# A first chunk of keys ahead of the query weights: reordering and splitting loads in a one-core decode kernel

## The chip, the cores and the metric

The kernel runs on one core of a Trainium2 chip. The metric is the device time of one execution, in microseconds; several runs are made and their median is given. The core has engines that run side by side, each with an instruction list of its own: PE (matrix products), DVE (vector work), ACT (activations), POOL, and SP, which here does nothing but issue transfers. Sixteen DMA engines move the data between HBM and the on-chip memory. They are fed by queues, and a queue works its transfers off in the order in which they were issued.

## The reference: one decode step of a transformer block

The input is a single token, `x` of 512 values. The step is attention over a long cache and then a gated feed-forward layer, each on the normalized input and added to it:

```
q = layernorm(x) @ wq                       # 32 query heads of 128
scores = q . k / sqrt(128)                  # 8 key heads, each serves 4 query heads, 65536 keys
o = softmax(scores) . v
h = x + o @ wo                              # wq is 512 x 4096, wo is 4096 x 512
out = h + (sigmoid(g) * u) @ w_down         # g, u = layernorm(h) @ w_gate, @ w_up ; F = 1792
```

All data are bf16. The keys and values of one head are 16 MiB each, 256 MiB for the eight heads. There is one query token, so each byte of the cache is read once and used for four query heads.

## The kernel before: how the work is tiled and staged

The cache of a head is cut into 32 *chunks* of 2048 keys, 512 KB each; `CH` is the length of one chunk in a partition. A chunk has 128 partitions with 16 keys of 128 values in each. Chunks live in a buffer called `ring`, which has room for 36 of them. A head's keys come in two halves, chunks 0 to 15 and 16 to 31 (`PIECES`), and so do its values. In a load of one half, partition p holds 256 keys that follow each other in memory, so its row is 64 KB long; which key lies in which partition and chunk follows from that (`rows` in `load`, L337). Keys and values must agree on this, since the weights of the softmax come out in the order of the keys.

`load(k, h, q, deps, sem, name, cols)` issues one transfer on SP's queue: head h, half q, chunks `cols` of it. `deps` are what SP waits for before it issues, `sem` the semaphore that counts the landing, `name` what others wait for. SP's list begins with wq (L341), which goes into `ktw`, and the keys of head 0 in four transfers of eight chunks (K0.0a, K0.0b, K0.1a, K0.1b). The first DMA in SP's list is placed ahead of the entry code of the program (L195 to L202). Then, for h from 1 to 7, come K*h*.0, V*(h-1)*.0, K*h*.1, V*(h-1)*.1, each waiting until its part of the ring is free: the marks `F` of DVE (L534) say that keys are used up, the names `PV` of PE that values are.

For each chunk DVE transposes the keys from `ring` into one of eight buffers in `ktw` (L531), and PE multiplies them with the head's query weights (`head_weights`, L500, a copy that ACT makes into the last part of `ktw`). Since wq lies in `ktw` too, the first transposes wait until the projection of the queries has read it. Within a head the chunks are taken in the order `ORDER = (*range(4, 16), *range(4), *range(16, 32))`. PE's four score matrices of a head stay in PSUM; `softmax(h)` has DVE find the maxima, ACT the exponentials (L577) and, as the last step, ACT copies the query weights of head h+1. The copy counts on a semaphore of its own ("W"), and PE's first scores of head h+1 wait for it. PE's work on the values of head h (`pv`) runs between the score blocks of head h+1; it waits for `V{h}.0` and `V{h}.1`. PE and DVE run the heads in loops, so the waits inside must be alike for all heads; ACT's and SP's lists are written out in full.

After the last head come the output projection and the feed-forward layer, whose weights are loaded into the same buffers at the end of SP's list (L354 to L374).

Of the kernel before, what the change touches and what calls it, by code (L numbers as in the profile page):

```python
# [9 lines left out]
AF = mybir.ActivationFunctionType  # L10
# [10 lines left out]
TC = 16  # L21
# [14 lines left out]
class Prog:  # L36
# [14 lines left out]
    def op(self, eng, fn, deps=(), name=None, to=None, times=1):  # L51
        assert name is None or name not in self.where, name
        self.ops[eng].append(dict(fn=fn, deps=[d for d in deps if d], name=name, dma=None, to=to, times=times, part=self.part.get(eng)))
        if name:
            self.where[name] = (eng, len(self.ops[eng]) - 1)

    def dma(self, eng, fn, sem, deps=(), name=None):
        self.op(eng, fn, deps, name)
        rec = self.dma_sems.setdefault(sem, dict(sem=None, count=0))
        rec["count"] += 16  # L60
        self.ops[eng][-1]["dma"] = (sem, rec["count"])
# [162 lines left out]
def bass_sequential_preLN__gqa_block_cached__glu_gated_glu__decode_kernel(  # L224
# [10 lines left out]
    CH = TC * DH  # L235
    PIECES = ((0, 16), (16, 32))
# [10 lines left out]
    with ExitStack() as es:  # L247
        def sb(name, shape, dt):
            return es.enter_context(nc.sbuf_tensor(name, shape, dt))
# [14 lines left out]
        ring = sb("ring", [128, RING], bf16)  # L264
# [4 lines left out]
        qz = sb("qz", [128, 8 * 64], bf16)  # L269
# [45 lines left out]
        def ps(bank, c0, c1, p0=0, p1=128):  # L315
            return PS[p0:p1, bank * 512 + c0: bank * 512 + c1]
# [5 lines left out]
        op, dma = P.op, P.dma  # L322
# [7 lines left out]
        def first_chunk(k, h, q):  # L330
            return AT[{("K", 0): "K0", ("V", HKV - 1): "V7"}.get((k, h), k)][q]

        def load(k, h, q, deps, sem, name, cols=None):
            j0, j1 = PIECES[q]
            a, z = cols or (j0, j1)
            cache = A_k_cache if k == "K" else A_v_cache
            rows = cache[0, h, j0 * TC * 128:j1 * TC * 128, :].rearrange("(p t) d -> p (t d)", p=128)  # L337
            at = (first_chunk(k, h, q) - j0) * CH
            dma("sp", lambda e: e.dma_start(ring[:, at + a * CH:at + z * CH], rows[:, (a - j0) * CH:(z - j0) * CH]), sem, deps, name)  # L339

        dma("sp", lambda e: e.dma_start(ktw[:, 0:NKT * CH].rearrange("p (k n) -> p k n", k=4),  # L341
                                        A_wq.rearrange("(p k) n -> p k n", p=128)), "r0", (), "wq")
        for q in range(2):
            for i in range(2):
                j0 = 16 * q + 8 * i
                load("K", 0, q, (), f"r{2 * q + i + 1}", f"K0.{q}{'ab'[i]}", (j0, j0 + 8))
        for h in range(1, HKV):
            load("K", h, 0, ["F0.0" if h == 1 else f"F{h - 1}.1"], "ka", f"K{h}.0")
            load("V", h - 1, 0, ["F0.1" if h == 1 else f"PV{h - 2}.3"], "va", f"V{h - 1}.0")
            load("K", h, 1, [f"F{h}.0"], "kb", f"K{h}.1")  # L350
            load("V", h - 1, 1, [f"PV{h - 1}.1"], "vb", f"V{h - 1}.1")
        h = HKV - 1
# [11 lines left out]
        for k, w in (("wg", B_w_gate), ("wu", B_w_up)):  # L364
            src = w.rearrange("(p k) n -> p (k n)", p=128)
            for i, (k0, k1) in enumerate(W_SPLIT[k]):
                at = W_AT[k]
                dma("sp", lambda e, at=at, w=src, a=k0 * FF, z=k1 * FF: e.dma_start(ring[:, at + a:at + z], w[:, a:z]),  # L368
                    f"{k}{i}", [f"PV{HKV - 1}.1"] if k == "wg" else (), f"{k}.{i}")
        src = B_w_down.rearrange("(p r) n -> p r n", p=128)  # L370
        for i, (r0, r1) in enumerate(WD_SPLIT):
            at = AT["wd"] * CH
# [123 lines left out]
        def head_weights(h):  # L496

            dst = bass.AP(tensor=ktw, offset=W0 + NC - 1, ap=[[KTW_ROW, 128], [WJ, 4], [NC, 16]])
            src = bass.AP(tensor=qz, offset=64 * h, ap=[[512, 128], [16, 4], [1, 16]])
            op("act", lambda e: e.activation(dst, src, AF.Copy), ["qz", "Wz"] if h == 0 else (), f"W{h}", to="W")  # L500

        def clear_out(h):

            op("act", lambda e: e.activation(ps(PO, 0, 512), bass.AP(tensor=zcol, offset=0, ap=[[1, 128], [0, 512]]), AF.Copy),  # L504
               ["zcol"] if h == 0 else (), f"z{h}", to="po")

        head_weights(0)
        clear_out(0)

# [4 lines left out]
        def dve_block(b):  # L514
            h, r = b // NR, b % NR
            for c in range(NC):
                n, s = b * NC + c, r * NC + c
                j = ORDER[s]
                q = sum(j >= z for _, z in PIECES)
                at = (first_chunk("K", h, q) + j - PIECES[q][0]) * CH  # L520
                src = ring[:, at:at + CH].bitcast(fp32)
                dst = ktw[:, (n % NKT) * CH:(n % NKT + 1) * CH].bitcast(fp32)
                if h == 0:
                    deps = [f"K0.{q}{'ab'[j % 16 // 8]}"] if s in (0, 4, 16, 24) else []
                    if s == 0:
                        deps.append("q")
                else:
                    deps = [f"K{h}.{q}"] if s in (0, 16) else []
                if r:
                    deps.append(f"S{b - 1}.{c}")  # L530
                op("dve", lambda e, d=dst, sr=src: e.transpose(d, sr), deps, f"T{b}.{c}", to="T")  # L531
                mark = ({15: 0, 31: 1} if h == 0 else {11: 0, 27: 1}).get(s)
                if mark is not None:
                    op("dve", lambda e, m=4 * h + mark: e.memset(scr[:, m:m + 1], 0.0), (), f"F{h}.{mark}")  # L534
            if b % NR == NR - 1:
                for k in range(NR):
                    u = b - NR + 1 + k
                    op("dve", lambda e, u=u: e.tensor_reduce(M_sb[:, u % 4:u % 4 + 1], ps(u % NS, 0, 512), AX.X, ALU.max),  # L538
                       [f"S{b}.{NC - NR + k}"], f"mx{u}", to="D")
                op("dve", lambda e: e.memset(scr[:, 32 + b // NR:33 + b // NR], 0.0), (), f"G{b // NR}")  # L540
# [19 lines left out]
        def softmax(h):  # L560
            k = h % 2
            op("dve", lambda e: e.tensor_reduce(gm[:, :], M_sb[:, :], AX.X, ALU.max),
               [f"mx{NR * h + r}" for r in range(NR)], f"gm{h}", to="g")
            op("pe", lambda e: e.matmul(ps(MISC, 0, 128, 0, 1), lhsT=gm[:, :], rhs=identf[:, :], start=True, stop=True),  # L564
               [f"gm{h}"], f"gmT{h}", to="Q")
            op("dve", lambda e: e.tensor_reduce(gmj[:, :], ps(MISC, 0, 128, 0, 1).rearrange("p (i a c) -> p a i c", a=4, c=NC),  # L566
                                                AX.XY, ALU.max), [f"gmT{h}"], f"gmj{h}", to="D")
            op("dve", lambda e: e.tensor_copy(gmrep[:, :].rearrange("p (i a c) -> p i a c", a=4, c=NC),  # L568
                                              bass.AP(tensor=gmj, offset=0, ap=[[4, 1], [0, 4], [1, 4], [0, NC]])),
               [f"gmj{h}"], f"gmrep{h}", to="g")  # L570
            op("pe", lambda e: e.matmul(ps(MISC, 128, 129), lhsT=gmrep[0:1, :], rhs=one_f[0:1, 0:1], start=True, stop=True),  # L571
               [f"gmrep{h}"], f"neg{h}")
            op("act", lambda e: e.activation(negmax[:, k:k + 1], ps(MISC, 128, 129), AF.Copy, scale=-att_scale),  # L573
               [f"neg{h}"], f"negmax{h}")
            for r in range(NR):
                b = NR * h + r
                op("act", lambda e, b=b: e.activation(P_sb[:, (b % 4) * 512:(b % 4 + 1) * 512], ps(b % NS, 0, 512), AF.Exp,  # L577
                                                      bias=negmax[:, k:k + 1], scale=att_scale,
                                                      accum_out=L_sb[:, b % 4:b % 4 + 1]), [f"negmax{h}"],
                   f"E{b}", to="E")  # L580
            if h + 1 < HKV:
                head_weights(h + 1)
# [259 lines left out]
        for i, (nm, bank) in enumerate((("wg", GB), ("wu", UB))):  # L842
            at = W_AT[nm]
# [73 lines left out]
```

## Time and profile before

| | |
|---|---|
| time, median of 3 runs | 656.33 us (656.27 to 656.40) |
| the profiled execution | span of 655.0 us from its first to its last instruction |
| PE busy | 397.5 us (61%) |
| DVE busy | 350.3 us (53%) |
| ACT busy | 43.1 us (7%) |
| moved by DMA | 282.33 MB, mean 431 GB/s over the span |
| mean clock granted to PE | 0.786 of full speed |

The page of the profile gives the busy time of each engine, the transfers, and the chain of work that ended last, followed back from the last instruction. Lines are those of the kernel (L531 is the transposes). "SPq" is SP's sequencer issuing a transfer. A transfer has two times: that of its issue, which is short, and that of its landing, when all its data are there and those who wait for it may go on. The views in order of time give the start of a piece first and then its length; windows give busy time of each engine between two times, the clock granted to PE, the mean share of the DMA engines that was busy, and the rate. All times are in microseconds from the first instruction of the profiled execution.

### The profile page before, as it was taken

Reading aid. Unit: us, or ns where it says so; the run is one execution under the profiler, and the core shown is the slowest. Engines: PE = TensorE matmul, PEld = TensorE weight load, DVE = VectorE, ACT = ScalarE, POOL = GpSimd, SP = SyncE. Lnnn points to the kernel's source line nnn. Section 1 sums busy time; section 2 is a strip of 40 time slices with the busy share of each in tenths; the row PEclk is TensorE's granted clock in tenths of the full one; section 3 lists DMA queues with packets and bytes.
Section 4 is the critical chain, followed back from the end, with each engine's and each line's share of the span. In section 5 each row is a group of like instructions: output and inputs, shape, how many; then the busy total and the mean of one; then the engine's idle time right before and its main releaser. Section 6 shows DMA issues by size and latency. Waiting matters only on the chain.

```text
span 655.0 us, 6176 instructions
## 1 busy us (share of the span) xinstructions
PE 397.5 (61%) x2317; PEld 66.7 (10%) x1549; DVE 350.3 (53%) x428; ACT 43.1 (7%) x114; POOL 3.7 (1%) x19
## 2 busy tenths in 40 slices
PE   2778672937548293674828467392845739285466
PEld 1100010110101000010100101010010101001122
DVE  3398853819266290935719184481917548092202
ACT  1100200020000200002000200002000020001101
POOL 1000000000000000000000000000000000000000
PEclk9799695977959687785968769596796958878656
DMA  9999999999999999999999999999999989999998
GB/s 400 432 434 462 424 408 448 448 448 412 420 448 448 432 400 448 448 448 404 428 448 448 436 396 448 448 448 416 416 448 448 448 384 448 448 448 424 417 412 363
DMA packets 6372, 282.33 MB, mean 431 GB/s; under 512 B 738, under 2 KB 868, under 8 KB 1252
## 3 DMA queue, kind: packets, MB, share of 16 engines
q1 hardware_dynamic: 6340, 282.33, 99.7%
q10 hardware_dynamic: 32, 0.00, 0.0%
HBM read 282.33 MB, written 0.00 MB: 431 GB/s over the span
## 4 chain that ended last, share of the span: by engine, by line
DMA 66%; DVE 30%; PE 2%; issue 1%; SPq 0%; PEldq 0%
DMA ring<-in_A_k_cache_dram 58%; DVE ktw L531 30%; DMA ring<-in_B_w_up_dram 4%; DMA ring<-in_A_v_cache_dram 4%; PE PS L443 2%; PE PS L866 0%; PE PS L847 0%; DVE hh L859 0%; DVE hhT L863 0%; SPq L368 0%; SPq L339 0%; DVE y_sb L884 0%; PEldq L171 0%
## 5 line engine op out<-in xcount | busy, mean ns | idle before, releaser
L531 DVE STREAM_TRANSPOSE ktw<-ring 128x1024 f32<-128x1024 f32 x256 | 291.5, 1208 | 165.0 <-DMA ring<-in_A_k_cache_dram 165.0
L443 PE MATMUL PS<-ktw 128*128 128x512 bf16 x1024 | 276.3, 419 | 163.4 <-DVE ktw L531 155.8
L443 PE MATMUL PS<-ring,PT_sb 128*32 x1024 | 85.0, 420 | 55.0 <-issue 46.6
L443 PEld LDWEIGHTS PS<-ktw 128*128 x256 | 26.2, 102 | 401.5 <-issue 234.3
L618 ACT ACTIVATE po_sb<-PS,rl 128x512 bf16<-128x512 f32 x8 | 5.5, 687 | 523.4 <-PE PS L443 523.4
L443 PEld LDWEIGHTS PS<-ring,PT_sb 128*32 x1024 | 20.7, 116 | 117.5 <-issue 116.2
L566 DVE TENSOR_REDUCE gmj<-PS 1x4 f32<-1x128 f32 x8 | 2.2, 278 | 53.5 <-PE PS L564 53.5
L538 DVE TENSOR_REDUCE M_sb<-PS 128x1 f32<-128x512 f32 x32 | 19.9, 683 | 19.3 <-PE PS L443 19.3
L577 ACT ACTIVATE P_sb<-PS,negmax 128x512 bf16<-128x512 f32 x32 | 21.6, 686 | 0.3
L587 DVE STREAM_TRANSPOSE PT_sb<-P_sb 128x512 bf16<-128x512 bf16 x32 | 19.9, 674 | 1.7 <-ACT P_sb L577 1.7
L443 PE MATMUL PS<-ktw,xz 128*8 x32 | 9.6, 476 | 6.1 <-DMA ktw<-in_A_wq_dram 6.1
L634 DVE TENSOR_TENSOR Lw<-O,blk_of 128x896 bf16<-128x896 bf16 (+1 forms) x2 | 1.4, 682 | 15.9 <-ACT O L624 15.9
L489 DVE STREAM_TRANSPOSE qt<-qh 32x512 bf16<-32x512 bf16 x1 | 0.7, 699 | 14.8 <-ACT qh L486 14.8
L571 PE MATMUL PS<-one_f,gmrep 1*128 1x1 f32 x16 | 4.7, 358 | 5.0 <-DVE gmrep L568 5.0
L564 PE MATMUL PS<-identf,gm 128*1 128x128 f32 x16 | 4.5, 380 | 5.1 <-issue 2.9
L643 DVE CAST O<-PS 128x28 bf16<-128x28 f32 (+1 forms) x2 | 0.3, 174 | 12.8 <-PE PS L640 12.8
L577 ACT ACTIVATION_READ_ACCUMULATOR P_sb<-PS,negmax 128x1 f32 x32 | 6.5, 203 | 0.0
L621 PE MATMUL PS<-sel_bf,po_sb 128*128 128x4 bf16 x32 | 2.1, 170 | 6.3 <-ACT po_sb L618 6.3
L504 ACT ACTIVATE PS<-zcol 128x512 f32<-128x512 bf16 x8 | 5.0, 622 | 0.0
L573 ACT ACTIVATE negmax<-PS 128x1 f32<-128x1 f32 x8 | 1.4, 171 | 54.0 <-PE PS L571 54.0
L571 PEld LDWEIGHTS PS<-one_f,gmrep 1*128 1x128 f32 x16 | 4.0, 307 | 8.8 <-DVE gmrep L568 8.8
L592 PE MATMUL PS<-L_sb,lsel 128*128 128x4 f32 x16 | 2.5, 229 | 3.8 <-DVE PT_sb L587 3.8
(90 smaller groups left out, 65.4 us busy)
## 6 DMA issues: line engine op xcount, KB each, us to landing
ring<-in_A_k_cache_dram SPq DMA_DIRECT2D x4, 4096.0 KB, 34.8
ring<-in_A_v_cache_dram SPq DMA_DIRECT2D x1, 5120.0 KB, 30.1
ktw<-in_A_wq_dram SPq DMA_DIRECT2D x1, 4096.0 KB, 12.2
ktw<-in_A_wo_dram SPq DMA_DIRECT2D x1, 3584.0 KB, 18.4
ring<-in_A_v_cache_dram SPq DMA_DIRECT2D x1, 3072.0 KB, 36.9
ring<-in_B_w_gate_dram SPq DMA_DIRECT2D x1, 1792.0 KB, 23.4
ring<-in_B_w_up_dram SPq DMA_DIRECT2D x1, 1792.0 KB, 27.2
ring<-in_B_w_down_dram SPq DMA_DIRECT2D x1, 1024.0 KB, 29.2
```

Of the source, the lines that this page charges most:

```text
L443: return e.add_instruction(mybir.InstMatmult(name=nc.get_next_instruction_name(), engine=mybir.EngineType.PE, ins=[rhs, lhsT], outs=[e.low ...
L504: op("act", lambda e: e.activation(ps(PO, 0, 512), bass.AP(tensor=zcol, offset=0, ap=[[1, 128], [0, 512]]), AF.Copy), ["zcol"] if h == 0 e ...
L531: op("dve", lambda e, d=dst, sr=src: e.transpose(d, sr), deps, f"T{b}.{c}", to="T")
L538: op("dve", lambda e, u=u: e.tensor_reduce(M_sb[:, u % 4:u % 4 + 1], ps(u % NS, 0, 512), AX.X, ALU.max), [f"S{b}.{NC - NR + k}"], f"mx{u}" ...
L564: op("pe", lambda e: e.matmul(ps(MISC, 0, 128, 0, 1), lhsT=gm[:, :], rhs=identf[:, :], start=True, stop=True), [f"gm{h}"], f"gmT{h}", to="Q")
L566: op("dve", lambda e: e.tensor_reduce(gmj[:, :], ps(MISC, 0, 128, 0, 1).rearrange("p (i a c) -> p a i c", a=4, c=NC), AX.XY, ALU.max), [f" ...
L571: op("pe", lambda e: e.matmul(ps(MISC, 128, 129), lhsT=gmrep[0:1, :], rhs=one_f[0:1, 0:1], start=True, stop=True), [f"gmrep{h}"], f"neg{h}")
L577: op("act", lambda e, b=b: e.activation(P_sb[:, (b % 4) * 512:(b % 4 + 1) * 512], ps(b % NS, 0, 512), AF.Exp, bias=negmax[:, k:k + 1], sca ...
L587: op("dve", lambda e, b=b: e.transpose(PT_sb[:, (b % 4) * 512:(b % 4 + 1) * 512], P_sb[:, (b % 4) * 512:(b % 4 + 1) * 512]), [f"E{b}"], f" ...
L592: op("pe", lambda e: e.matmul(ps(MISC, 132, 136), lhsT=lsel[:, :], rhs=L_sb[:, :], start=True, stop=True), [f"PT{NR * h + NR - 1}"], f"l{h ...
L618: op("act", lambda e: e.activation(po_sb[:, :], ps(PO, 0, 512), AF.Copy, scale=rl[:, :]), [f"PV{h}.{NR - 1}", f"rl{h}"], f"po{h}", to="po")
L621: op("pe", lambda e, t=t: e.matmul(ps(OX, 0, 4), lhsT=po_sb[:, t * 128:(t + 1) * 128], rhs=sel_bf[:, 8 * t:8 * t + 8:2], start=(t == 0), s ...
```

## The change

The first half of head 0's keys is assigned anew: chunk 0 is now the first 2048 keys, one contiguous block of 512 KB with 4 KB in each partition, and chunks 1 to 15 are the 30720 keys behind it, with 60 KB of consecutive keys in each partition. The order within the softmax doesn't matter as long as the values follow, so the first half of head 0's values is assigned in the same way.

Chunk 0 of the keys, `K0.0c`, becomes a transfer of its own and the first in SP's list, ahead of wq. `K0.0a` then has seven chunks (1 to 7) in place of eight. `V0.0` becomes two transfers, `V0.0c` (chunk 0) and `V0.0` (chunks 1 to 15), one right after the other. DVE's transpose of chunk 0 waits for `K0.0c`, and ACT's copy of the query weights of head 1 (`W1`) waits for `V0.0c`.

```diff
             at = (first_chunk(k, h, q) - j0) * CH
-            dma("sp", lambda e: e.dma_start(ring[:, at + a * CH:at + z * CH], rows[:, (a - j0) * CH:(z - j0) * CH]), sem, deps, name)
-
+            c0 = j0
+            if h == q == 0:
+                first = TC * 128
+                c0, keys = (0, (0, first)) if z == 1 else (1, (first, PIECES[0][1] * TC * 128))
+                rows = cache[0, h, keys[0]:keys[1], :].rearrange("(p t) d -> p (t d)", p=128)
+            dma("sp", lambda e: e.dma_start(ring[:, at + a * CH:at + z * CH], rows[:, (a - c0) * CH:(z - c0) * CH]), sem, deps, name)
+
+        load("K", 0, 0, (), "r5", "K0.0c", (0, 1))
         dma("sp", lambda e: e.dma_start(ktw[:, 0:NKT * CH].rearrange("p (k n) -> p k n", k=4),
                                         A_wq.rearrange("(p k) n -> p k n", p=128)), "r0", (), "wq")
         for q in range(2):
             for i in range(2):
                 j0 = 16 * q + 8 * i
-                load("K", 0, q, (), f"r{2 * q + i + 1}", f"K0.{q}{'ab'[i]}", (j0, j0 + 8))
+                load("K", 0, q, (), f"r{2 * q + i + 1}", f"K0.{q}{'ab'[i]}", (max(j0, 1), j0 + 8))
         for h in range(1, HKV):
             load("K", h, 0, ["F0.0" if h == 1 else f"F{h - 1}.1"], "ka", f"K{h}.0")
-            load("V", h - 1, 0, ["F0.1" if h == 1 else f"PV{h - 2}.3"], "va", f"V{h - 1}.0")
+            if h == 1:
+                load("V", 0, 0, ["F0.1"], "vc", "V0.0c", (0, 1))
+            load("V", h - 1, 0, ["F0.1" if h == 1 else f"PV{h - 2}.3"], "va", f"V{h - 1}.0", (1, 16) if h == 1 else None)
...
-            op("act", lambda e: e.activation(dst, src, AF.Copy), ["qz", "Wz"] if h == 0 else (), f"W{h}", to="W")
+            op("act", lambda e: e.activation(dst, src, AF.Copy), ["qz", "Wz"] if h == 0 else ["V0.0c"] if h == 1 else (), f"W{h}", to="W")
...
                     if s == 0:
                         deps.append("q")
+                    if j == 0:
+                        deps.append("K0.0c")
```

## The prediction

> **What bounds the kernel now.** I read the page first, for the share of each engine and for the chain of work that ended last.
>
> ```profile
> span 655.0 us, 6176 instructions
> PE 397.5 (61%) x2317; PEld 66.7 (10%) x1549; DVE 350.3 (53%) x428; ACT 43.1 (7%) x114; POOL 3.7 (1%) x19
> DMA packets 6372, 282.33 MB, mean 431 GB/s; under 512 B 738, under 2 KB 868, under 8 KB 1252
> q1 hardware_dynamic: 6340, 282.33, 99.7%
> DMA 66%; DVE 30%; PE 2%; issue 1%; SPq 0%; PEldq 0%
> ktw<-in_A_wq_dram SPq DMA_DIRECT2D x1, 4096.0 KB, 12.2
> ```
>
> No compute engine is busy for more than 61% of the span, while the one queue that SP feeds keeps the sixteen DMA engines occupied for 99.7% of it. The chain is two thirds DMA. Its other third, DVE, needs a second look: it could mean that DVE sets when transfers are issued and that the queue then runs dry. The chain in order of time shows how the two interlock:
>
> ```profile
> 1.31 30.32 DMA ring<-in_A_k_cache_dram
> 45.34 24.98 DMA ring<-in_A_k_cache_dram
> 84.16 24.75 DMA ring<-in_A_k_cache_dram
> ...
> 108.93 13.67 DVE ktw L531 x13
> ...
> 547.86 24.73 DMA ring<-in_A_k_cache_dram
> 572.61 13.70 DVE ktw L531 x13
> ...
> 621.60 27.22 DMA ring<-in_B_w_up_dram
> ```
>
> The first number is the start, the second the length. A half head of keys (8 MiB) lands, DVE works through enough of it to free the ring, SP issues the next half, and 24.7 to 25.0 us later that one lands. Landings at 70.32 (45.34 + 24.98) and 572.59 (547.86 + 24.73) are 13 such periods apart: 38.64 us for 16 MiB of keys and values, or 434 GB/s. Is that the DMA engines' limit or the loop's? An idle queue answers it. wq, 4 MiB, is the first transfer and lands 12.2 us after its issue. Its bytes at 434 GB/s are 9.66 us, so latency alone is about 2.5 us. Then 8 MiB issued into an empty queue would land after 19.32 + 2.5 = 21.9 us. The keys take at least 24.73, so every issue finds **about 2.9 us of earlier work still queued**. The queue never runs dry, and DVE's 30% are time in which the engines were working off that backlog. The stretches by window say the same:
>
> ```profile
> core 0: us, PE busy (x) PEld busy (x) DVE busy (x) ACT busy (x) POOL busy (x), PEclk, DMA share, GB/s
> 2.75:12.00 9.25, 0.79 (x3) 0.60 (x3) 3.66 (x19) 0.71 (x2) 1.20 (x4) 1.00 1.05 450
> 12.00:30.00 18.00, 12.73 (x40) 3.57 (x35) 5.20 (x5) 3.24 (x7) 0.00 (x0) 0.86 0.99 430
> 30.00:50.00 20.00, 15.61 (x63) 1.58 (x16) 18.35 (x18) 0.00 (x0) 0.00 (x0) 0.95 0.99 429
> 70.00:590.00 520.00, 315.17 (x1778) 46.80 (x1115) 292.10 (x328) 31.43 (x88) 0.00 (x0) 0.78 1.00 434
> 649.00:651.00 2.00, 2.00 (x18) 0.78 (x10) 0.85 (x2) 0.00 (x0) 0.00 (x0) 0.50 0.98 412
> 651.50:652.25 0.75, 0.55 (x24) 0.58 (x28) 0.72 (x3) 0.00 (x0) 0.00 (x0) 0.50 1.03 395
> 1.00:1.75 0.75, 0.00 (x0) 0.00 (x0) 0.42 (x3) 0.69 (x1) 0.73 (x6) 1.00 2.54 699
> ```
>
> The last two columns are the DMA share and rate. A packet's time counts in the window where it starts, so short windows overshoot and the rate is to be divided by the share. From 70 to 590 us: share 1.00, 434 GB/s. The end hangs on the last weights that land (the up weights at 621.60 + 27.22 = 648.82) and on 6 us of work behind them. So the time is bytes over rate, plus a fixed head and tail. The change can move it by (a) moving the first byte, (b) making the bytes slower, or (c) opening a gap, which a delay has to outgrow 2.9 us to do.
>
> **The change part by part.** The bytes are unchanged. Two transfers of 512 KB are split off, K0.0c (first of all) and V0.0c (ahead of V0.0).
>
> *Packets.* 6372 packets fit one per partition row and transfer, plus one small completion packet per engine and transfer. So each new transfer brings 128 data packets of 4 KB, 8 per engine, and a completion on each. Rows of 28 and 60 KB replace rows of 32 and 64 KB; their count stays. The trace holds no 4 KB packets from the cache. The nearest rows are the down weights at the end: 3 KB packets run at 395 / 1.03 = 383 GB/s, which is 0.128 us each on one engine against 0.113 at 434 GB/s, 15 ns extra; around 649 to 651, mostly 8 KB packets, 412 / 0.98 = 420 GB/s gives 10 ns. I take 15 ns, since 4 KB lies next to 3 KB: 16 packets per engine, **+0.24 us**. The lower end is nothing: K0.0b's landing at 31.63 (1.31 + 30.32) to K1.0's at 70.32 is 38.69 us for 16 MiB, half of it in 32 KB rows, within 0.05 us of the steady period in 64 KB rows. The upper end is a whole latency of 2.5 us for each transfer, not overlapped; I keep it as a rival.
>
> *The head of the queue.* SP's issues:
>
> ```profile
> 0.00 0.40 SPq L341 DMA_DIRECT2D ktw<-in_A_wq_dram  x1
> 0.93 2.14 SPq L339 DMA_DIRECT2D ring<-in_A_k_cache_dram  x4
> 63.41 0.33 SPq L339 DMA_DIRECT2D ring<-in_A_v_cache_dram  x1
> 84.16 0.33 SPq L339 DMA_DIRECT2D ring<-in_A_k_cache_dram  x1
> ```
>
> The first DMA of SP's list is put ahead of the entry code; that place goes from wq to K0.0c. A plain cache load takes 0.33 us to issue and wq 0.40, so the first packets, which began between 1.00 and 1.75 us, may come 0.07 us earlier: **-0.07 us**. They took 2.54 x 0.75 = 1.9 us where 32 KB at 434 GB/s is 1.21; the 0.7 us of start-up is paid once in either order. If it were filling a 32 KB packet, up to 0.6 us could be gained; if a 4 KB start leaves it alone, nothing. I take nothing. wq is now issued from 0.93 on, so by its own example its packets can begin at 1.9 to 2.7 us. K0.0c occupies each engine until about 1.0 + 0.7 + 8 x 0.166 = 3.0 us at the earliest. The queue has its next work at least 0.3 us in time; were this cover gone, the gap would be at most the 0.93 us between the two issues. The four K0 loads are issued some 0.5 us later each (2.14 us for four), for data that is due many microseconds on. Nothing.
>
> *wq and the queries.* wq lands 8 x 0.166 = 1.33 us later, less 0.07: 1.26 us. The projection waits for wq, head 0's first transposes wait for the projection, because wq lies in their buffer.
>
> ```profile
> 12.95 9.64 PE L443 MATMUL PS<-ktw,xz 128*8 x32 [6.05 <-DMA ktw<-in_A_wq_dram]
> 24.10 4.57 DVE L531 STREAM_TRANSPOSE ktw<-ring 128x1024 f32<-128x1024 f32 x4
> 26.57 1.61 PE L443 MATMUL PS<-ktw 128*128 128x512 bf16 x3 [3.76 <-ACT ktw L500]
> 28.72 4.72 PE L443 MATMUL PS<-ktw 128*128 128x512 bf16 x14 [0.54 <-DVE ktw L531]
> 31.65 14.81 DVE L531 STREAM_TRANSPOSE ktw<-ring 128x1024 f32<-128x1024 f32 x13 [2.98 <-DMA ring<-in_A_k_cache_dram]
> ```
>
> DVE does four transposes and then sits idle 2.98 us until K0.0b lands. It will start them at 25.4, end at 29.9 and still wait: K0.0b has the same bytes ahead of it as before (0.5 + 4 + 3.5 + 4 MiB). PE's first scores, at half clock and up to 33.44, end at about 34.7; the first transpose that needs a buffer back comes at 31.65 + 4 x 1.14 = 36.2. Hidden, with 1.5 us to spare; beyond that 2.9 us of backlog. So the wq delay costs nothing, and nothing starts earlier either: head 0 is worked in the order of chunks 4 to 15, then 0 to 3, so chunk 0, the one brought forward, is the thirteenth. DVE's new wait for it, and the transposes queued behind, find it long landed.
>
> *Values of head 0.* V0.0c and V0.0 are issued from 63.41, one issue (0.5 us) more, while K1.0 lands only at 70.32; nothing. V0.0c comes right behind K1.0 in the queue, so it lands at about 70.32 + 1.33 = 71.65. The new wait is on ACT, ahead of the weights of head 1's scores:
>
> ```profile
> 70.34 14.93 DVE L531 STREAM_TRANSPOSE ktw<-ring 128x1024 f32<-128x1024 f32 x13 [0.90 <-DMA ring<-in_A_k_cache_dram]
> 72.33 0.69 ACT L577 ACTIVATE P_sb<-PS,negmax 128x512 bf16<-128x512 f32 x1
> 72.99 0.49 ACT L500 ACTIVATE ktw<-qz 128x64 bf16<-128x64 bf16 x1
> 73.63 14.33 PE L443 MATMUL PS<-ktw 128*128 128x512 bf16 x51 [3.54 <-ACT ktw L500]
> ```
>
> ACT comes to that copy only at 72.99, after the four exponentials; 1.3 us of cover. If V0.0c is later than that, PE's first scores of head 1 wait with ACT, then DVE for its buffers, then K1.1's issue at 84.16, and there the 2.9 us of backlog begin to be eaten. ACT has nothing else due until the output of head 0. Nothing.
>
> **Sum:** 0.24 - 0.07 = +0.17 us. The profiled execution has a span of 655.0 us, 1.33 below the median of the runs, 656.33; the start and end around the span aren't touched. 656.33 + 0.17 = **656.5 us**.
>
> **The rivals.**
>
> *Slower: a gap per added transfer.* At the edge of each new 512 KB transfer the engines stand still for the 2.5 us that wq showed beyond its bytes. Two of them: 656.33 + 5.1 = 661.4; one alone, where K0.0c drains before wq's packets exist, 658.8. It decides from 1.3 us, a quarter of it. Against it: the 70 to 590 us stretch runs over many transfer edges at share 1.00; 2.5 us lost per 8 MiB would need 8.39 MB / 16.8 us = 499 GB/s in between. For it: no transfer as short as 1.2 us stands in the steady part. The Trainium skill ("DMA: Bandwidth & Descriptors", "Anatomy of one DMA — SWDGE (gpsimd) path", and its "Rules for kernel authors") puts a fixed part of about 2.0 us on every DMA of the GpSimd path and asks for 1 MiB or more; by that alone the sum would be about 660.3, an estimate. The steady share of 1.00 disagrees with paying it one after the other.
>
> *Slower: a delay breaks through the backlog.* If V0.0c landed after 72.99 + 2.9 + 1.3 = 77.2 us rather than 71.65, the keys of head 1 would be issued so late that the queue empties and 1.3 us are lost: 657.6 and up. It would have to be overtaken by the 8 MiB queued behind it. The mechanism is real, the size unlikely.
>
> *Faster: the cache rows are no longer a power of two apart.* 15 chunks of K0 and 15 of V0.0, 15.7 MB, now lie at a pitch of 60 KB in place of 64 KB. If the even pitch slows reading, those bytes speed up. By the best slice on the page:
>
> ```profile
> GB/s 400 432 434 462 424 408 448 448 448 412 420 448 448 432 400 448 448 448 404 428 448 448 436 396 448 448 448 416 416 448 448 448 384 448 448 448 424 417 412 363
> ```
>
> 462 against 434 GB/s is 36.2 - 34.0 = 2.2 us: 654.1. Against it: wq, one block of contiguous 32 KB rows, ran at 450 / 1.05 = 429 GB/s between 2.75 and 12 us, no faster than the 64 KB pitch; the slices' steps are whole packets. The Trainium skill (same page, "Latency and other measured facts", the row on pitches at large powers of two) has copies at a pitch of 512 KiB and up slowed, and a few KiB of padding as a cure in one case; the 434 GB/s here at 64 KB show no such loss.
>
> **How the numbers follow.** The likeliest, the bytes at the same rate with 16 small packets more per engine, has 0.83. A gap at a transfer's edge has 0.06, a broken backlog 0.04, the pitch 0.07. Within 0.2% (1.3 us, about what a measurement of this kernel can tell from no change) lie the likeliest and its unknowns: -0.6 - 0.07 us for the start-up, up to 0.9 for a late wq. So same 0.83, slower 0.10, faster 0.07. The range takes in those bounds, with a little room for the rivals' small versions: 655.4 to 657.6.
>
> **What would show it.** Right: a DMA share of 1.00 and 434 GB/s from 70 to 590 us; K0.0b landing at 31.6 to 31.9 and K1.0 at 70.2 to 70.7; DVE still idle before K0.0b, by about 1.7 us; ACT's copy for head 1 still directly behind the fourth exponential; issue to landing of the later keys still near 24.9. Wrong: a hole in the DMA share between 2.5 and 4 us (a gap), the head 1 copy waiting for V0.0c (the wait), a period of the key landings other than 38.6 us after head 1, or K0's and V0's landings early by a microsecond or more (the pitch).

## The result, and the profile after

The changed kernel took 658.60 us in the median (657.92 to 660.19), beside 656.44 for the kernel before: a ratio of 1.0034 with an interval from 1.0024 to 1.0044. It is slower by 2.2 us, outside the range of the prediction (655.4 to 657.6), and it scatters over 2.3 us where the kernel before stays within 0.45. The profiled execution is the slowest of the six (660.19 us); their spans run from 655.8 to 657.9. One execution among those below, of the kernel with 61 extra rows, was disturbed (752.6 us) and is left out of that kernel's figures.

These are lines of the page of the changed kernel, and from its list of transfers the row of K0.0c (the columns are the size, and the time from issue to landing):

```profile
span 657.9 us, 6179 instructions
DMA packets 6660, 282.33 MB, mean 429 GB/s; under 512 B 770, under 2 KB 900, under 8 KB 1540
q1 hardware_dynamic: 6628, 282.33, 99.4%
ktw<-in_A_wq_dram SPq DMA_DIRECT2D x1, 4096.0 KB, 15.4
ring<-in_A_k_cache_dram SPq DMA_DIRECT2D x1, 512.0 KB, 3.5
```

The packets are the ones that were counted: 288 more, 256 of them of 4 KB. wq is the row to look at. It was 12.2 us before and is 15.4 now, from an issue that is 0.93 us later. It lands at 16.3 us, where 0.5 MiB more ahead of it would make it 12.2 + 1.2 = 13.4. The chain in order of time tells whether these 2.9 us stay (start, length):

```profile
1.78 32.66 DMA ring<-in_A_k_cache_dram
...
48.15 24.99 DMA ring<-in_A_k_cache_dram
86.86 24.98 DMA ring<-in_A_k_cache_dram
111.86 13.67 DVE ktw L541 x13
...
550.65 24.84 DMA ring<-in_A_k_cache_dram
575.51 13.76 DVE ktw L541 x13
...
624.42 27.31 DMA ring<-in_B_w_up_dram
```

Landing by landing against the kernel before: K0.0b 34.44 and 31.63 (2.8 late), K1.0 73.14 and 70.32 (2.8), the last half head of keys 575.49 and 572.59 (2.9), the up weights 651.73 and 648.82 (2.9). **The whole loss is there before the first keys are used, and it is carried unchanged to the end.** From issue to landing the keys still take 24.8 to 25.0 us, and the period is the same. The windows of before, then of after, agree (the last columns are DMA share and GB/s):

```profile
1.00:9.00 8.00, 0.79 (x3) 0.60 (x3) 5.05 (x22) 2.39 (x3) 2.92 (x14) 1.00 1.04 410
```

```profile
1.00:9.00 8.00, 0.77 (x3) 0.60 (x3) 5.04 (x22) 2.39 (x3) 2.93 (x14) 1.00 0.99 352
70.00:590.00 520.00, 312.76 (x1769) 46.99 (x1116) 290.84 (x331) 31.41 (x88) 0.00 (x0) 0.78 1.00 434
```

In the first 8 us of traffic 0.46 MB less gets started, and from 70 to 590 us it is 434 GB/s as before. The DMA share of the first window hardly falls, since it counts the time of packets that have started, and these became longer.

What the 16 engines did can be read from the trace's records of single packets. A record doesn't name its engine; I joined each packet to the one that ended just before it. (Where several engines stand still, this doesn't tell which pause belongs to which engine; how many stand still at a time doesn't depend on it.) The two kinds of engine found in the third set of runs of the changed kernel (bytes, start + length in us):

```
in time:  4096@2.46+0.16  32768@2.62+1.29  32768@3.90+1.23  32768@5.13+2.02  32768@7.15+1.27
run dry:  4096@2.52+0.16  (nothing for 2.2 us)              32768@4.90+1.84  32768@6.73+1.21
```

After its eight packets of K0.0c, between 2.6 and 3.1 us, an engine either finds wq's first packet waiting or stands still: eight engines in the first profile (0.6 to 2.0 us each), two in the second (some 2 us each), nine in the third (one for 0.3, eight for 1.5 to 2.3 us). The first packet after the pause is also slow, mostly 1.4 to 2.9 us for what takes 1.21 otherwise.

The rest went as the prediction had it. DVE still waits for K0.0b, and ACT's copy for head 1 follows the fourth exponential at once:

```profile
34.46 11.38 DVE L541 STREAM_TRANSPOSE ktw<-ring 128x1024 f32<-128x1024 f32 x10 [2.24 <-DMA ring<-in_A_k_cache_dram]
```

```profile
75.07 0.69 ACT L587 ACTIVATE P_sb<-PS,negmax 128x512 bf16<-128x512 f32 x1
...
75.73 0.50 ACT L508 ACTIVATE ktw<-qz 128x64 bf16<-128x64 bf16 x1
```

### The profile page after: what moved, and what is told of

Read it like the earlier page. It is cut to its first block, busy times and chain, and to the rows that moved or that the text cites. A ratio compares the mean times of both kernels' runs of the same rounds, so it can differ in the third digit from the quotient of the medians.

```text
span 657.9 us, 6179 instructions
## 1 busy us (share of the span) xinstructions
PE 397.1 (60%) x2317; PEld 66.6 (10%) x1549; DVE 350.2 (53%) x428; ACT 43.1 (7%) x114; POOL 3.7 (1%) x19
## 3 DMA queue, kind: packets, MB, share of 16 engines
q1 hardware_dynamic: 6628, 282.33, 99.4%
## 4 chain that ended last, share of the span: by engine, by line
DMA 66%; DVE 30%; PE 2%; issue 1%; SPq 0%; PEldq 0%
DMA ring<-in_A_k_cache_dram 58%; DVE ktw L541 30%; DMA ring<-in_B_w_up_dram 4%; DMA ring<-in_A_v_cache_dram 4%; PE PS L451 2%; PE PS L876 0%; PE PS L857 0%; DVE hh L869 0%; SPq L344 0%; DVE hhT L873 0%; SPq L376 0%; SPq L347 0%; DVE y_sb L894 0%; PEldq L171 0%
## 5 line engine op out<-in xcount | busy, mean ns | idle before, releaser
L644 DVE TENSOR_TENSOR Lw<-O,blk_of 128x896 bf16<-128x896 bf16 (+1 forms) x2 | 1.4, 682 | 16.1 <-ACT O L634 16.1
## 6 DMA issues: line engine op xcount, KB each, us to landing
ktw<-in_A_wq_dram SPq DMA_DIRECT2D x1, 4096.0 KB, 15.4
```

## The experiments

The theory (G in the expectations): K0.0c is drained before wq's packets are there, engines run dry, and starting them again is dear. Rivals: the new rows cost the time (R), the new waits or V0.0c do (W), the contiguous block that all engines read at once does (H), or the small load of x on the other queue does.

**Order, size and part.** Four kernels, on one chip.

Order: wq back to first place, everything else of the change kept.

```diff
-        load("K", 0, 0, (), "r5", "K0.0c", (0, 1))
         dma("sp", ... wq ...)
+        load("K", 0, 0, (), "r5", "K0.0c", (0, 1))
```

> The changed kernel with the first two transfers in the other order: wq first (ahead of the entry code again), K0.0c behind it; the split, the contiguous assignment and both new waits stay. Theory G (a gap: K0.0c is drained before wq's packets are there): the gap is gone, wq's 9.7 us cover every later issue; 656.3 to 656.8 us, wq landing 12 to 13 us after its issue. Theory R (the new rows, 4 KB, 28 KB and 60 KB, cost the time wherever they stand): stays near 658.6 us. Theory W (one of the new waits, or V0.0c): stays near 658.6 as well.

656.38 us, ratio 1.000 (0.9991 to 1.001). wq lands after 12.2 us, as before:

```profile
span 655.1 us, 6179 instructions
ktw<-in_A_wq_dram SPq DMA_DIRECT2D x1, 4096.0 KB, 12.2
...
45.26 24.98 DMA ring<-in_A_k_cache_dram
```

All the packets, rows of 60 KB, new waits and V0.0c together cost nothing that shows; the interval is some 0.6 us to either side. R and W fall, and with them the pitch as a cause in either direction, unless a gain and a loss cancel.

Size: a first transfer of two chunks, then of four (`n` is 2 or 4; V0.0c alike).

```diff
-                first = TC * 128
-                c0, keys = (0, (0, first)) if z == 1 else (1, (first, PIECES[0][1] * TC * 128))
+                first = n * TC * 128
+                c0, keys = (0, (0, first)) if z == n else (n, (first, PIECES[0][1] * TC * 128))
...
-        load("K", 0, 0, (), "r5", "K0.0c", (0, 1))
+        load("K", 0, 0, (), "r5", "K0.0c", (0, n))
...
-                load("K", 0, q, (), ..., (max(j0, 1), j0 + 8))
+                load("K", 0, q, (), ..., (max(j0, n), j0 + 8))
```

> The changed kernel with a first transfer of two chunks (1 MB, 8 KB rows) in place of one, keys and values alike. Theory G: the first transfer keeps the engines 1.2 us longer, so of a gap of up to 2 us on the late engines some 1.2 us are covered: 656.5 to 657.6 us. Theory R: the number of small packets is unchanged, only their size doubles: 658.0 to 658.6.

> The changed kernel with a first transfer of four chunks (2 MB, 16 KB rows). Theory G: 3.6 us more cover than with one chunk, beyond the whole gap: 656.3 to 656.8 us, with no hole in the DMA share before 8 us. Theory R: near 658. If it is not the drain time but that the transfer that is first has not been wq (the place in the list), it stays near 658.6.

Two chunks: 656.82 us, ratio 1.0003 (0.9993 to 1.0013). Four: 656.82, 1.0012 (1.0002 to 1.0022), with single runs up to 658.3. With two chunks the engines are busy with the first transfer until 4.3 to 4.5 us, and every engine goes on to wq without a pause. wq's issue is as late as in the changed kernel, and its place in the list the same; it is the drain time that counts. The row of wq with two chunks first:

```profile
ktw<-in_A_wq_dram SPq DMA_DIRECT2D x1, 4096.0 KB, 13.6
```

The remainder with four chunks is not a gap: no engine pauses there either. wq lands at 17.5 us, 5.3 us later than before, and then the projection is too late for DVE, which begins its first four transposes at 29.35 instead of 24.10 and no longer waits for K0.0b. The slack for a late wq is used up, and the chain of this run begins with wq and the projection (start, length):

```profile
0.93 16.57 DMA ktw<-in_A_wq_dram
...
86.46 22.95 DMA ring<-in_A_k_cache_dram
```

The keys of the second line are issued at 86.46 us instead of 84.16, 2.3 us late, and land at 109.41 instead of 108.91, 0.5 us late. So queued work covers most of a late issue here; it doesn't cover time that engines have lost.

Part: the key split alone, with the keys assigned as before (4 KB pieces 64 KB apart), no V0.0c, no new wait on ACT.

```diff
+        load("K", 0, 0, (), "r5", "K0.0c", (0, 1))
         dma("sp", ... wq ...)
...
-                load("K", 0, q, (), ..., (j0, j0 + 8))
+                load("K", 0, q, (), ..., (max(j0, 1), j0 + 8))
...
+                    if j == 0:
+                        deps.append("K0.0c")
```

> The kernel before with one part of the change alone: chunk 0 of head 0's keys as a transfer of its own ahead of wq, but with the keys assigned as before (4 KB pieces 64 KB apart), and the values loaded in one transfer, no V0.0c and no wait on ACT. Theory G: the gap is there, 658.2 to 658.8 us. Theory R in its contiguous form (the new assignment), and theory W: 656.4 us.

656.62 us, ratio 1.0004 (0.9995 to 1.0014): a miss for G as I had put it, and what H and "the contiguous assignment" expected. In its profile K0.0c's strided packets are drained at 2.9 to 3.3 us, some 0.2 to 0.3 us later than the contiguous ones, and wq's packets follow on every engine without a pause:

```profile
ktw<-in_A_wq_dram SPq DMA_DIRECT2D x1, 4096.0 KB, 12.6
```

So either the contiguity matters by itself, or the edge lies within these 0.3 us (the ends of the drain that the later expectations name, 2.5 to 2.9 us, were read a little too low).

**Which of the two, and is it the chip?** The next four ran on another chip, with the changed kernel again as a base.

> The changed kernel once more, on the chip of this group, as the base for the three below. If its loss belongs to the kernel: 657.9 to 660.2 us and a stretch before 8 us in which part of the engines stand still. If it belongs to the chip on which it ran first: 656.4 to 656.8.

659.54 us (658.77 to 660.77), ratio 1.0040 (1.0027 to 1.0054). The loss is there again.

wq's issue put ahead of the entry code too:

```diff
-        first = self.ops["sp"].pop(0)
-        ...
+        for _ in range(2):
+            first = self.ops["sp"].pop(0)
+            ...
```

> The changed kernel with wq's issue also put ahead of the entry code, so that SP issues it about 0.4 us after the start and not 0.93; rows, order and waits stay. Theory G (wq's packets come a fraction of a microsecond after K0.0c is drained, and an engine that has run dry takes 1 us and more to start again): half a microsecond earlier is enough for most or all engines, 656.3 to 657.0 us. Theory H (the contiguous block of 512 KB, read by all engines at once, is what slows the packets that follow it): no change, near 658.6.

656.73 us, ratio 1.0004 (0.9994 to 1.0013); single runs reach 658.15, but no span is over 655.7. These are the issues of SP (start, length), the changed kernel first, then this one:

```profile
0.00 0.40 SPq L344 DMA_DIRECT2D ring<-in_A_k_cache_dram  x1
0.93 0.33 SPq L347 DMA_DIRECT2D ktw<-in_A_wq_dram  x1
1.30 3.00 SPq L344 DMA_DIRECT2D ring<-in_A_k_cache_dram  x4
```

```profile
0.00 0.40 SPq L345 DMA_DIRECT2D ring<-in_A_k_cache_dram  x1
0.45 0.41 SPq L348 DMA_DIRECT2D ktw<-in_A_wq_dram  x1
1.27 1.85 SPq L345 DMA_DIRECT2D ring<-in_A_k_cache_dram  x4
```

Issued 0.48 us earlier, wq is in time for all engines. The rows, the contiguous block and the order are those of the changed kernel, so H falls.

Half a chunk first, strided (the run with the key split, `(0, 0.5)` for the first transfer and `max(j0, 0.5)` for K0.0a):

> The run with the key split alone (keys assigned as before, values in one piece), its first transfer halved to 256 KB, 2 KB rows 64 KB apart. Theory G: it drains some 0.6 us earlier than the whole chunk, before wq's packets are there, so engines run dry although nothing is contiguous: 657.5 to 660 us. Theory H: nothing contiguous, 656.4 to 656.8.

658.19 us, ratio 1.0026 (1.0016 to 1.0035). Nothing is contiguous, and engines run dry, because the 2 KB packets are through at 1.8 to 2.5 us. This and the run before it settle G against H.

The load of x in ACT's own list instead of ahead of the entry code:

```diff
-        first = self.ops["act"].pop(0)
-        ...
```

> The changed kernel with the 1 KB load of x taken from ahead of ACT's entry code and issued in ACT's own list, some 0.8 us later. If x's small packets on the second queue are what holds the engines up between the two first transfers, the loss changes by a microsecond or vanishes (656.5), or grows; theories G and H both: no change beyond 0.5 us, near 658.6.

658.25 us (656.76 to 659.1), ratio 1.0025 (1.0016 to 1.0034). The loss stays, if smaller. In its profile x's packets run from 3.8 us on, when K0.0c is through on every engine, and two engines stand still all the same, so x's packets are not needed for the loss. SP's issues also shifted (wq at 0.81), so the smaller loss doesn't tell whether they have some part in the odds.

wq's landing against the time at which it was due (12.2 us plus the bytes ahead of it at 434 GB/s) accounts for nearly all of each profile's excess in span (the kernel before itself ranges from 654.8 to 655.7). The exception is the run with wq issued sooner: its 0.6 us come later, with K1.0, which takes 25.56 us from issue to landing.

| first transfer | wq issued | wq landed | due | late | span over 655.0 |
|---|---|---|---|---|---|
| wq (before) | 0.00 | 12.2 | 12.2 | 0 | 0 |
| 512 KB (the change) | 0.93 | 16.3 | 13.4 | 2.9 | 2.9 |
| the same, again | 0.93 | 16.1 | 13.4 | 2.7 | 2.8 |
| the same, third set | 0.93 | 15.6 | 13.4 | 2.2 | 2.1 |
| x later | 0.81 | 15.2 | 13.4 | 1.8 | 1.9 |
| 256 KB, strided | 0.93 | 14.7 | 12.8 | 1.9 | 2.0 |
| 512 KB, strided | 0.93 | 13.5 | 13.4 | 0.1 | 0.3 |
| 512 KB, wq issued sooner | 0.45 | 13.2 | 13.4 | -0.2 | 0.6 |
| 1 MB | 0.93 | 14.5 | 14.6 | -0.1 | 0 |

The packet records tie the lateness to the last engine. The last of the sixteen to finish its first packet of wq does so at 7.51, 6.98 and 6.78 us in the three profiles of the changed kernel, at 6.36 with x later, at 5.71 with 256 KB first, and at 3.43 in the kernel before. In every profile of the table wq lands 8.7 to 9.2 us after that moment, however many engines were late.

**What running dry costs, by itself.** The kernel before, where SP issues K0.0a only after wq has landed:

```diff
-                load("K", 0, q, (), ...)
+                load("K", 0, q, ["wq"] if q == i == 0 else (), ...)
```

> The price of running dry, by itself: the kernel before (wq first, nothing split), with one edit, that SP issues K0.0a only when wq has landed. All sixteen engines stand still once. From the trace of before, wq's landing comes 2.5 us after its bytes would be through by the rate alone, and that is what an issue into an empty queue loses: 656.4 + 2.5 = 658.9 us, all of it visible as K0.0b landing about 2.5 us later. If the 2.9 us of queued work swallowed such a gap, as they do with late DVE work, it would be 656.4.

659.49 us (659.28 to 659.57), ratio 1.0046 (1.0032 to 1.0061), 3.2 us. Lines of its page and chain:

```profile
span 658.0 us, 6176 instructions
...
12.56 21.38 DMA ring<-in_A_k_cache_dram
...
47.77 24.86 DMA ring<-in_A_k_cache_dram
```

K0.0b lands at 33.94, 2.3 us late, and K1.0 at 72.63, 2.3 us late. That is near the expected 2.5. Part of the other 0.7 us of the span comes in with one load of keys, issued at 202.25 us, that takes 25.38 us to land; behind it the lateness is 2.8 us. Why is open. The backlog swallows none of it. By the packet records the engines stood still for 1.7 us on the average, SP's wait for the landing included, and the first packet of 15 of them took 1.5 to 2.0 us instead of 1.21.

**Is one late engine enough?** In the second profile of the changed kernel only two engines stood still, yet the span was 2.8 us longer. The kernel before, with an extra load that nobody reads behind K0.1b:

```diff
+        dma("sp", lambda e: e.dma_start(ring[0:61, 17 * CH:17 * CH + 512], ...), "ex", (), "extra")
         for h in range(1, HKV):
...
-            load("K", h, 1, [f"F{h}.0"], "kb", f"K{h}.1")
+            load("K", h, 1, [f"F{h}.0", "extra" if h == 1 else None], "kb", f"K{h}.1")
```

> Whether one late engine is enough: the kernel before with one extra load behind K0.1b, 61 rows of 1 KB from another head into a free chunk of the ring that nobody reads, only that chunk's next load waits for it. If a transfer of 61 rows goes to a single one of the sixteen engines, that engine gets 61 x 0.046 = 2.8 us more work (0.046 us for a 1 KB packet, from the down weights at the end of before). Theory S (a transfer has landed only when the slowest engine is through, every engine has the same share of every load, so one late engine delays the whole rest): 659.0 to 659.4 us. If the lateness of one is shared out among the sixteen: 2.8 / 16 = 0.2, 656.6.

The three runs took 665.95 to 670.79 us, ratio 1.0171 (1.0138 to 1.0205): far more than either side expected. There is no profile of these three, so where the 10 us went is open. I repeated it with the packet size of the changed kernel and with half of that, 17 rows instead of 61:

> The extra load once more, with packets of the size that stood in the changed kernel: 17 rows of 4 KB behind K0.1b, read by nobody. If 17 rows go to one engine, that engine gets 17 x 0.159 = 2.7 us of extra work. Theory S (the slowest engine sets every landing): 656.4 + 2.7 = 659.1 us, range 658.8 to 660. Shared out: 656.6. If it costs 9 us or more, as the 61 rows of 1 KB did, then a late engine costs more than its lateness, and S names only part of it.

> The same with 17 rows of 2 KB: 17 x 0.084 = 1.4 us on one engine. Theory S: 657.8 us, range 657.5 to 658.5, half the loss of the 4 KB rows. Shared out: 656.5.

4 KB: 660.61 us, ratio 1.0066 (1.0049 to 1.0083), 4.2 us, above the range that S had. 2 KB: 658.03, ratio 1.0023 (1.0012 to 1.0033), 1.6 us, within it. K1.0, behind the extra load in the queue, in the two chains:

```profile
45.25 28.51 DMA ring<-in_A_k_cache_dram
```

```profile
45.48 26.02 DMA ring<-in_A_k_cache_dram
```

It lands at 73.76 and 71.50, 3.4 and 1.2 us late. The packet records show the 17 packets one after the other, from 50.23 to 53.76 and from 50.32 to 51.68: one engine, 3.5 and 1.4 us. The later packets of the 4 KB run took up to 0.34 us and not 0.16, which the expectation didn't have; packets of 64 KB on other engines took 2.6 to 3.0 us and not 2.42 in that stretch. Shared out among sixteen engines these loads would cost 0.1 to 0.2 us. So the slowest engine sets the landings, and its lateness is not given back. The Trainium skill ("DMA: Bandwidth & Descriptors", "Why a DMA increments its semaphore by 16 and not by 1") says that a transfer is spread over the largest number of engines up to 16 that divides its row count, which is one for 17 rows; the trace agrees.

At the end of the trace the engines show the same. Their last packets of the up weights end within 0.5 us of each other in the kernel before (648.0 to 648.5) and in the run with wq first (0.3 us), but 1.7 us apart in the changed kernel and 1.9 us in the run with 17 rows of 4 KB.

**The edge, on one chip.** The changed kernel had no run beside the first four, on their chip.

> The changed kernel, third time, beside the next two on one chip. If the loss belongs to the kernel: 658 to 660 us here too. If to the chip: 656.4 to 656.8.

> The key split alone with the keys assigned as before, again, on the same chip as the changed kernel. Theory G with the drain time as the edge (its strided packets drained at 3.0 to 3.3 us and not at 2.5 to 2.9): 656.4 to 656.9, with single runs up to a microsecond more where an engine runs dry after all. If the chip made the difference: 658 or more.

> The changed kernel with a first transfer of two chunks, on the same chip. Theory G: its engines are busy until 4.1 to 4.4 us, no gap on any chip: 656.3 to 657.0. If the chip made the difference: 658 or more.

On one chip: the change 658.96 us (ratio 1.0033, 1.0024 to 1.0043), the strided split 657.39 (1.0015, 1.0006 to 1.0025; single runs to 660.09), two chunks first 656.98 (1.0008, 0.9998 to 1.0017). It is not the chip. The strided split came out above the 656.4 to 656.9 us expected for it. Spans tell it run by run, since the kernel before has none over 655.7: of the changed kernel all 21 executions are over that (655.8 to 657.9), of the strided split 5 of 20 (up to 657.5), of two chunks first 1 of 20 (656.2). So the strided split is at the edge: mostly in time, sometimes not. The contiguous chunk, through 0.2 to 0.3 us sooner, by its spans never quite is. That the drain time is how contiguity acts is the reading that fits all runs; the records of one profile each are too few to show it run by run.

## Why the prediction was wrong

The step that failed is *the head of the queue*, in three places.

- "The queue has its next work at least 0.3 us in time": I compared the earliest start of wq's packets, carried over from an issue into an idle queue (1.0 to 1.8 us after it), with the end of K0.0c. The latter was 2.6 to 3.1 us, 2.7 to 2.8 in the mean over the engines, and not 3.0 at the earliest: the 0.7 us of start-up, taken over from 32 KB packets, was too much for 4 KB packets, some of whose first took 0.16 us like any other. And on up to nine engines wq's first packet began 2.3 to 4.0 us after wq's issue at 0.93. A latency measured on idle engines is no bound for a second issue on running ones, and I had no row for that.
- "were this cover gone, the gap would be at most the 0.93 us between the two issues": engines stood still for up to 2.3 us, and the next packet took up to 2.90 us instead of 1.21. The bound counted the distance of the issues and left out the restart. In the strided split wq was issued at the same 0.93, and its packets followed on every engine at 2.9 to 3.3 us; starts as late as 4.9 us belong to engines that had run dry.
- The engines were treated as one. A mean over sixteen hides two that are late, and two were enough. The sign that was named for a gap, a hole in the DMA share between 2.5 and 4 us, doesn't show: the share there is 0.88 before and 0.86 after.

The rival that came true was written down with its place and its price: "one alone, where K0.0c drains before wq's packets exist, 658.8"; 658.60 was measured. It had a chance of 0.06 together with its larger form. That the price came so near is in part luck: it had every engine stand still for 2.5 us, where two to nine did, for 0.3 to 2.3 us and a slow packet behind it. What was set against it, the steady stretch at share 1.00, says only that a transfer issued long ahead of time costs nothing at its edge. V0.0c shows that too; it says nothing on the first edge, the only one without a backlog ahead of it.

What held, and the smaller terms:

- The bytes, the rate of 434 GB/s and the period of 38.6 us are unchanged, and a late start is carried to the end one to one (2.8, 2.8, 2.9, 2.9 us).
- The small packets: 0.159 us for 4 KB against 0.151, 8 ns extra and not 15, so 0.13 us in place of 0.24. The row taken for 3 KB packets holds 2 KB ones too, and the trace of before has 128 packets of 4 KB, of wo, at 0.159 us each, which the prediction passed over. The run with wq first, which has all of them, shows 0.
- -0.07 us for a shorter first issue: none. K0.0c took 0.40 us to issue in the first place and wq 0.33 in the second, so the 0.40 goes with the place.
- The wait for V0.0c: landed at 66.22 + 8.1 = 74.3, needed at 75.73; the cover was 1.4 us where 1.3 was worked out.
- wq late for DVE: 3.55 us later at its first transposes (27.65 against 24.10) and still hidden, because K0.0b is late by nearly the same. In the four-chunk run, where it is 5.3 us, it is not hidden. (PE's clock for the first scores was not half throughout: 0.50 for three of them, 0.67 in the mean for the next 14. Nothing hung on it.)
- The pitch of 60 KB: no gain and no loss beyond the 0.6 us of the interval, by the run with wq first.

## To carry to other kernels

Where a kernel lives on a DMA queue that never empties, the one place where it is empty is the start. The first transfer had to last until the second had reached every engine: 512 KB, through at 2.6 to 3.1 us, was too short for an issue at 0.93 us, 1 MB was enough, and so was issuing the second at 0.45. Look at transfers by engine and not by mean share: with two of sixteen engines late the span was 2.8 us longer, and the share of the queue read 99.4% instead of 99.7%.

## What the runs showed of the hardware

- First packets of the first transfer begin 1.02 us after the start, 0.62 us after SP's issue ends. The Trainium skill ("DMA: Bandwidth & Descriptors", "Latency and other measured facts") has about 0.6 us to the first byte for such an issue, which agrees if it is counted from the issue's end. The second issue here was slower: its packets came 2.3 to 4.0 us after it where an engine had run dry.
- One engine's extra 1.4 us cost the kernel 1.6 us, an extra 3.5 us cost 4.2; 61 packets of 1 KB on one engine cost some 10 us, which nothing here explains.
- Engines that did not run dry in the first and third profile of the changed kernel had one slow packet as well, their third of wq, with 1.9 to 2.4 us instead of 1.21, at about 5.2 us, while the others were starting. Its cause is open; in the profile with two late engines it hardly appears.
- The profiled execution of the changed kernel took 2.3 us beside its span (660.19 and 657.9), two others of the first six 2.0 and 2.1, the remaining three 1.3; before it was 1.33. So part of the scatter lies outside the span, and no profile shows what it is.
